# Six PSUM banks handed out one by one by a build-time scheduler, in place of two fixed PSUM pools, in a block-sparse attention and MLP kernel

## Chip, cores and metric

The kernel runs on one core of one Trainium2 chip. The metric is the device time of one execution in microseconds (us). One core has TensorE (PE; PEld is its weight load), VectorE (DVE), ScalarE (ACT), GpSimd (POOL) and SyncE (SP). PSUM is the memory that this kernel's matmuls write and that its VectorE and ScalarE instructions read. A run is called fast or slow by its clock and time; unless said otherwise, fast runs are compared with fast runs. Time before the change: 314.98 us in the first three runs.

## The reference, cut to what matters

```python
# attention: batch 4, 8 heads, sequence 768, head size 64, blocks of 32
scores = (q @ k.T) / 8
scores = where(block_mask, scores, -1e9)        # band, first/last blocks, sampled blocks
attn   = softmax(scores);  x = attn @ v          # -> x [4, 768, 512]
# residual MLP
a1  = alpha1 * x + beta1
u   = x + lam * (w_tok @ a1)                     # token mixing, 768 x 768
a2  = alpha2 * u + beta2
out = u + lam * (relu(a2 @ w_ch1) @ w_ch2)       # channel mixing, 512 -> 2048 -> 512
```

## The kernel before, as far as the change and the argument touch it

The kernel writes its program with a list scheduler that runs in Python while the kernel is built. Each piece of work is a `Job` with an engine, a guessed duration, a priority, and slots that it takes and gives back. The scheduler decides the order of instructions on every engine. A separate build tool then places the semaphore waits, and in the programs built here it placed them by tile (220 of 234 of PE's waits in the changed kernel, below).

Sixteen pairs of heads are processed. A PSUM bank is here 512 fp32 columns, as the kernel cuts it. A unit of scores is 128 x 1024 fp32, so it fills two banks. The scores of pairs 0 to 5 contract 88 rows (64 and 24 for the mask). Those of pairs 6 to 15 contract 64 rows, with the two heads of a pair side by side in rows 0 to 63 and 64 to 127 of the operands; in the trace of before the second head's matmul starts 3 to 4 ns after the first's (L729). The program uses eight PSUM banks:

```python
# two score tiles of 2 banks, two single tiles, one for channel mixing, one for attention @ v
def mm_tile(shape, dt=FP):
    return ps.tile(shape, dt, name="mm", tag="mm", bufs=2)
...
sps = ps.tile([P, UN], FP, name="sps", tag="sps", bufs=2)     # a new tile for every unit
...
slots = dict(sps=2, mm=2, cp=1, ops=1, eT=NET, ...)
...
# scores of pairs 6 to 15: always two units in one group
jq = Job("PE", 2 * 225.0 + 175.0, (1, i0), qk, deps, take=("sps", "sps"), give=give)
# exp of one unit frees its score tile
je = Job("ACT", 950.0, (1, i), ex, [qk_jobs[i]], take=("eT",), give=("sps",), lat=160.0)
# first channel matmul: a single product in an mm tile (later also half a score tile)
...
# scores may run ahead of channel mixing by LEAD units
def gated(j):
    return j.gate is not None and j.gate >= NS and j.gate - NS > st["ch"] / rate + LEAD
```

The softmax here doesn't subtract the row's maximum and nothing guards it: scores larger than these inputs give would overflow.

## Time and profile before

| what | before |
|---|---|
| time, median of the first 3 runs | 314.98 us (314.65 to 318.46) |
| PE busy | 305.6 us, 97% of the span |
| PE gaps (all pauses of PE together) | 5.2 us in 11 gaps |
| matmul streaming, columns / 2.4 + 2.7 ns each (a fit, below), summed | 290.3 us |
| what the start-to-start times add to that | 19.0 us |
| groups of 64-row scores | 45, all of two units |

The streaming sum and the excess were worked out from the start times of all 3197 matmuls; two heads that stream side by side count once. The form is a fit to this trace: the median from start to start is 56 ns at 128 columns and 216 ns at 512, so 160 ns for 384 columns, 2.4 columns a ns, and 2.7 ns more for each matmul. At 256 and 384 columns, with medians of 109 and 162 ns, the fit is off by less than 1 ns. Every matmul has its weight load here (3197 of each).

Lines of the page of the kernel before: busy time, then PE's busy tenths and the granted clock in 40 slices of the span.

```profile
span 314.2 us, 7579 instructions
...
PE 305.6 (97%) x3197; PEld 187.3 (60%) x3197; DVE 213.7 (68%) x447; ACT 198.1 (63%) x259; POOL 51.8 (16%) x91
...
PE   7999999988999999999999999999999999999995
...
PEclk9999999999999999999999999999999999999999
```

PE is the bottleneck. Its granted clock is 1.00 in the records from 6.0 to 313.2 us, and its last matmul ends at 310.7 us. (No record covers the first 6.0 us, in which the `warm` matmuls of 512 columns start 400 to 427 ns apart.) The two longest of PE's waits in the same kernel (who waited for whom: us in total, times, longest):

```profile
PE mm L946 <- DVE x_sb L874: 2.4, 1, 2.4
PE cp L170 <- DVE warm L165: 1.2, 1, 1.2
```

Timeline of before (start us, duration, engine, line, operation, count), one group of 64-row scores (L729):

```profile
152.08 1.03 PE L997 MATMUL cp<-w2b,hts 128*128 128x512 bf16 x4
153.04 0.61 PE L729 MATMUL sps<-qx,kx 64*128 64x256 bf16 x6
153.58 0.29 PE L787 MATMUL ops<-vext,eT 128*128 128x65 f16 x4
```

Four matmuls of 512 columns take 4 x 216 = 864 ns, so the scores could start at 152.94 us; they start 96 ns later. The scores themselves stream for 435 ns, with about 10 ns more after their first pair, and the next matmul starts 96 ns after that. The changes from 128-row to 64-row matmuls and back (mode changes, below) cost 95 and 96 ns at the median of the 45 groups, 0.19 us a group.

The second stretch lies after attention, where first channel products (L946) fill three PSUM tiles in turn:

```profile
267.08 0.81 PE L946 MATMUL sps<-uT,w1b 128*128 128x384 bf16 x4
267.73 1.46 PE L946 MATMUL mm<-uT,w1b 128*128 128x384 bf16 x8
267.93 0.58 ACT L959 ACTIVATE hts<-sps,b1t 128x384 bf16<-128x384 f32 x1
268.58 1.23 ACT L959 ACTIVATE hts<-mm,b1t 128x384 bf16<-128x384 f32 x2
269.03 0.49 PE L946 MATMUL sps<-uT,w1b 128*128 128x384 bf16 x2
```

Three products start between 267.08 and 269.03 us, one each 0.65 us.

### The profile page before, as it was taken

The numbers are of one execution on the slowest core, as the hardware profiler recorded it, in microseconds if no ns is written. First come the engines' busy times: TensorE is split into PE (matmuls) and PEld (weight loads), VectorE is DVE, ScalarE is ACT, GpSimd is POOL, SyncE is SP. The second block draws the span as 40 slices with busy tenths as digits, with TensorE's granted clock in tenths as the row PEclk, the third lists the DMA queues.
The fourth block names the chain that finished last, engine by engine and source line by source line (L and its number), as shares of the span: only waits on it lengthen the run. The fifth ranks groups of instructions, "written<-read, shape, count | busy, mean of one in ns | idle before, by whom it ended". The sixth has DMA issues, their size and how long they took to land.

```text
span 314.2 us, 7579 instructions
## 1 busy us (share of the span) xinstructions
PE 305.6 (97%) x3197; PEld 187.3 (60%) x3197; DVE 213.7 (68%) x447; ACT 198.1 (63%) x259; POOL 51.8 (16%) x91
## 2 busy tenths in 40 slices
PE   7999999988999999999999999999999999999995
PEld 3687888764645655566646655565656565556444
DVE  4599988859888687788869787788859671010111
ACT  4999988975768664766577654766587502828000
POOL 5647332000211220220310220230000000000000
PEclk9999999999999999999999999999999999999999
DMA  6999999994254564625452665626110203010021
GB/s 153 181 250 206 209 204 213 178 116 92 37 98 78 69 118 100 120 49 113 87 102 26 108 113 109 111 40 120 37 28 1 59 35 92 0 69 0 34 101 67
DMA packets 47210, 30.81 MB, mean 98 GB/s; under 512 B 27552, under 2 KB 43080, under 8 KB 47176
## 3 DMA queue, kind: packets, MB, share of 16 engines
q0 software_dynamic: 15984, 15.47, 31.4%
q1 hardware_dynamic: 30940, 14.61, 20.1%
q8 instruction: 25, 0.41, 0.6%
q10 hardware_dynamic: 252, 0.24, 0.2%
q14 instruction: 9, 0.07, 0.1%
HBM read 32.04 MB, written 6.33 MB: 122 GB/s over the span
## 4 chain that ended last, share of the span: by engine, by line
PE 79%; DMA 12%; issue 3%; DVE 3%; POOL 1%; ACT 1%; POOLq 0%
PE mm L946 23%; PE cp L997 22%; DMA v<-in_v_dram 8%; PE ops L787 8%; PE sps L729 7%; PE mm L864 7%; PE ops L997 5%; DMA q<-in_q_dram 4%; PE sps L946 2%; PE cp L170 2%; PE sps L651 2%; PE ops L691 1%; DVE ot L1014 1%; POOL w2b L389 0%; PE mm L218 0%
## 5 line engine op out<-in xcount | busy, mean ns | idle before, releaser
L755 ACT ACTIVATE eT<-sps 128x1024 f16<-128x1024 f32 x90 | 88.3, 1020 | 31.1 <-PE sps L729 28.8
L946 PE MATMUL mm<-uT,w1b 128*128 128x384 bf16 (+1 forms) x468 | 88.8, 326 | 3.0 <-DVE x_sb L874 2.4
L959 ACT ACTIVATE hts<-mm,b1t 128x384 bf16<-128x384 f32 x82 | 47.7, 582 | 49.3 <-PE mm L946 47.2
L997 PE MATMUL cp<-w2b,hts 128*128 128x512 bf16 (+1 forms) x320 | 76.9, 374 | 0.2
L946 PEld LDWEIGHTS <-w1b 128*128 128x128 bf16 x512 | 46.4, 97 | 34.9 <-issue 6.4
L760 DVE TENSOR_TENSOR eT<-eT,maskT 128x1024 f16<-128x1024 f16 x90 | 60.5, 685 | 4.1 <-ACT eT L755 4.0
L997 PEld LDWEIGHTS <-hts 128*128 128x128 bf16 x400 | 36.8, 98 | 35.7 <-issue 2.1
L666 ACT ACTIVATE eT<-sps 128x1024 f16<-128x1024 f32 (+1 forms) x55 | 52.1, 1024 | 3.1 <-PE sps L651 2.8
L787 PEld LDWEIGHTS <-eT 128*128 128x128 f16 x720 | 29.9, 97 | 15.9 <-issue 5.6
L1014 DVE TENSOR_TENSOR ot<-x_sb,cp 128x512 f32<-128x512 f32 (+1 forms) x20 | 13.5, 673 | 37.0 <-PE cp L997 36.8
L864 PE MATMUL mm<-a1p,wtokT 128*128 128x128 bf16 x576 | 36.2, 219 | 0.0
L787 PE MATMUL ops<-vext,eT 128*128 128x65 f16 x720 | 35.5, 194 | 0.0
L864 PEld LDWEIGHTS <-wtokT 128*128 128x128 bf16 x576 | 33.0, 98 | 2.0 <-issue 0.4
L651 PE MATMUL sps<-qx,kx 88*128 88x512 bf16 (+1 forms) x144 | 31.6, 325 | 0.6 <-DVE rel L213 0.5
L314 POOL COPY held<-flag 1x1 bf16<-1x1 bf16 x24 | 9.2, 385 | 131.1 <-DVE flag L334 131.1
L963 DVE TENSOR_SCALAR hts<-mm,b1t 128x384 bf16<-128x384 f32 x35 | 21.6, 616 | 13.5 <-PE mm L946 13.2
L729 PE MATMUL sps<-qx,kx 64*128 64x512 bf16 (+1 forms) x240 | 27.3, 327 | 0.0
L874 DVE TENSOR_TENSOR x_sb<-x_sb,mm 128x384 f32<-128x384 f32 x32 | 17.7, 552 | 4.7 <-PE mm L864 4.3
L691 PEld LDWEIGHTS <-eT 128*128 128x128 f16 x432 | 18.2, 97 | 4.4 <-DVE x_sb L626 0.6
L691 PE MATMUL ops<-vext,eT 128*128 128x65 f16 x432 | 20.2, 193 | 0.0
L626 DVE TENSOR_TENSOR x_sb<-ops,rcp 128x384 f32<-128x384 f32 x32 | 17.9, 558 | 1.1
L729 PEld LDWEIGHTS <-kx 64*128 64x128 bf16 x240 | 8.1, 94 | 16.5 <-issue 14.1
(71 smaller groups left out, 237.2 us busy)
## 6 DMA issues: line engine op xcount, KB each, us to landing
out_dram<-ot SPq DMA_DIRECT2D x23, 256.0 KB
v<-in_v_dram POOLq DMA_DIRECT2D x16, 192.0 KB, 5.4
q<-in_q_dram POOLq DMA_DIRECT2D x15, 192.0 KB, 3.9
k<-in_k_dram POOLq DMA_DIRECT2D x15, 192.0 KB, 5.4
w1b<-in_moe_w_ch_dram POOLq DMA_DIRECT2D x4, 512.0 KB, 10.3
w2b<-in_moe_w_ch_dram POOLq DMA_DIRECT2D x4, 512.0 KB, 16.4
wtk<-in_moe_w_tok_dram POOLq DMA_DIRECT2D x3, 384.0 KB, 10.3
maskT<-mask_rows SPq DMA_DIRECT2D x14, 72.0 KB
```

The source lines that it names most:

```text
L651: nc.tensor.matmul(sps[:, f - u * UN : f - u * UN + w], kx[h][0:KC, ts(jt, P)], qx[h][0:KC, c : c + w], start=True, stop=True,)
L666: nc.scalar.activation(eT[:, c], sps[:, c], AF.Exp, bias=EXPB, scale=SCALE)
L691: nc.tensor.matmul(ops[p, a][:, t * VW : t * VW + D + 1], eTs[p, u][:, ts(i - u * GU, P)], vx[:, a, jt, 0 : D + 1], start=(i % HT == 0), s ...
L729: nc.tensor.matmul(sps[:, a * 512 + lo : a * 512 + lo + w], kx[sl][r, ts(jt, P)], qx[sl][r, c : c + w], start=True, stop=True,)
L755: nc.scalar.activation(eT[:], sps[:], AF.Exp, bias=EXPB, scale=SCALE)
L760: nc.vector.tensor_tensor(out=e, in0=e, in1=maskT[:, u, :].unsqueeze(1).broadcast_to([P, 2, 512]), op=ALU.min,)
L787: nc.tensor.matmul(ops[p, a][:, t * VW : t * VW + D + 1], eTs[p, u][:, a * 512 + c * P : a * 512 + (c + 1) * P], vx[:, a, jt, 0 : D + 1], ...
L864: nc.tensor.matmul(tp[:, j, :], wtokT[:, s, ts(3 * g + j, P)], tl["a1p", p][:, s, :], start=(s == 0), stop=(s == NT - 1),)
L946: nc.tensor.matmul(hp[:, 0:nc_], w1b[:, dk, ts(f, P)], uTs[b][:, dk, hf * HS : hf * HS + nc_], start=(dk == 0), stop=(dk == 3),)
L959: nc.scalar.activation(hts[kk][:, f, :], hp[:, 0:HS], AF.Relu, bias=b1t[:, f : f + 1], scale=1.0)
L963: nc.vector.tensor_scalar(out=hts[kk][:, f, :], in0=hp[:, 0:HS], scalar1=b1t[:, f : f + 1], scalar2=0.0, op0=ALU.add, op1=ALU.max,)
L997: nc.tensor.matmul(cps[kk, mi][:, 0:w], hts[kk][:, nk, ts(m, P)], w2tile[0][:, nk, lo : lo + w], start=(nk == 0), stop=(nk == 15),)
```

## The change

The intent: with 64-row scores in groups of three units instead of two, there are fewer mode changes. Three units need six banks, so all six banks that are neither `cp` nor `ops` become one shared store. The scheduler knows them as `b0` to `b5`, gives single products one bank and scores a pair of banks, and holds single products back for a moment when a third pair would come free, as long as PE has 800 ns of other work (`COVER`).

```diff
-LEAD = 15
+LEAD = 18
+COVER = 800.0
...
-    def mm_tile(shape, dt=FP):
-        return ps.tile(shape, dt, name="mm", tag="mm", bufs=2)
+    ps6 = ps.tile([P, 6 * 512], FP, name="ps6", tag="ps6", bufs=1)
+    BANKS = tuple(f"b{i}" for i in range(6))
+    PAIRS = ("b0+b1", "b2+b3", "b4+b5")
+
+    def bank(name, shape, dt=FP):
+        t = ps6[:, ts(BANKS.index(name), 512)]
+        ...
+    def two_banks(names):
+        return ps6[:, ts(PAIRS.index(names), UN)]
...
-        sps=2, mm=2, cp=1, ops=1, eT=NET, ...
+        **{b: 1 for b in BANKS}, cp=1, ops=1, eT=NET, ...
...
-                sps = ps.tile([P, UN], FP, name="sps", tag="sps", bufs=2)
+                sps = two_banks(tl.pop(("spsb", p, u)))
...
+    def qk_group(n, banks):              # n = 2 or 3 units, as free pairs allow
+        ...
+        j = Job("PE", n * 225.0 + 175.0, (1, i0), qk, (), take=take, give=give)
...
+                    hold[1] = not n or later
+                    hold[0] = n > m and not later and other_work(t) >= COVER
```

More of the change, by code (lines that the diff above doesn't have):

```diff
@@ L145, in pair_ap @@
         return src[b, 2 * n : 2 * n + 2].rearrange("h (p o) d -> p h (o d)", o=NT)
-    def mm_tile(shape, dt=FP):
-        return ps.tile(shape, dt, name="mm", tag="mm", bufs=2)
+    ps6 = ps.tile([P, 6 * 512], FP, name="ps6", tag="ps6", bufs=1)
[3 more added lines that the diff above has]
+        t = ps6[:, ts(BANKS.index(name), 512)]
+        if dt != FP:
+            t = t.bitcast(dt)
+        t = t[:, 0 : int(np.prod(shape[1:]))]
+        return t if len(shape) == 2 else t.rearrange("p (o c) -> p o c", o=shape[1])
+    def two_banks(names):
+        return ps6[:, ts(PAIRS.index(names), UN)]
     q2f = wk.tile([P, 2, NT * D], FP, name="q2f", tag="hts", bufs=2)
@@ L213, in first_cast, with transposes @@
                 nc.vector.tensor_copy(out=dst, in_=sl)
-    def transposes(rel, a, slots=range(NT)):
-        tps = mm_tile([P, NT, P], BF)
+    def transposes(rel, a, name, slots=range(NT)):
+        tps = bank(name, [P, NT, P], BF)
         for o in slots:
             nc.tensor.transpose(tps[:, o, :], rel[:, a, o, :], identb[:])
-        return tps[:].rearrange("p o c -> p (o c)")
+        return tps.rearrange("p o c -> p (o c)")
     first_cast(0)
     block_mask()
-    flatA = transposes(rel0, 0, range(0, 3))
-    flatB = transposes(rel0, 0, range(3, 6))
+    flatA = transposes(rel0, 0, "b0", range(0, 3))
+    flatB = transposes(rel0, 0, "b1", range(3, 6))
     bqs = []
-    for w, tag in ((0, "sps"), (1, "ops")):
-        t = ps.tile([P, UN if tag == "sps" else 512], FP, name=tag, tag=tag, bufs=2 if tag == "sps" else 1)
+    for w in range(2):
+        t = ps.tile([P, 512], FP, name="ops", tag="ops", bufs=1) if w else bank("b2", [P, 512])
         nc.tensor.matmul(
@@ L253 @@
     slots = dict(
-        sps=2, mm=2, cp=1, ops=1, eT=NET, head=NQB, vext=NV, ld=NLD, rel=3,
+        **{b: 1 for b in BANKS}, cp=1, ops=1, eT=NET, head=NQB, vext=NV, ld=NLD, rel=3,
         x=NXB, uT=3, hts=2, a1p=2, ub=2, ot=2, w2b=1,
@@ L272, in __init__ @@
             self.gate = None
+            self.marks = []
             self.n = len(jobs)
@@ L423, in tr @@
         def tr(t=t):
-            tl["wt", t] = tp = mm_tile([P, NT, P], BF)
+            tl["wt", t] = tp = bank(tl.pop(("wtb", t)), [P, NT, P], BF)
             for s in range(NT):
@@ L428, in cp_ @@
         def cp_(eng, t=t):
-            copy(eng, wtokT[:, :, ts(t, P)], tl.pop(("wt", t))[:])
-        j = Job("PE", mmt(NT, P), (5, t), tr, [wload["tok", t // 2]], take=("mm",))
+            copy(eng, wtokT[:, :, ts(t, P)], tl.pop(("wt", t)))
+        j = Job("PE", mmt(NT, P), (5, t), tr, [wload["tok", t // 2]], take=((BANKS, ("wtb", t)),))
         last = t == NT - 1
         wtok_jobs.append(
-            Copy((4, t), cp_, [j], give=("mm", "w2b") if last else ("mm",), only=False)
+            Copy((4, t), cp_, [j], give=(("wtb", t),) + (("w2b",) if last else ()), only=False)
         )
@@ L525, in f_tr @@
             def f_tr():
-                tl["h0"] = transposes(rel0, 1)
+                tl["h0"] = transposes(rel0, 1, tl.pop(("h0b",)))
             def f_cq(eng):
@@ L535 @@
             j = Job("DVE", 720.0, (2, 0), fc)
-            j = Job("PE", mmt(NT, P), (2, 0), f_tr, [j], take=("mm",))
+            j = Job("PE", mmt(NT, P), (2, 0), f_tr, [j], take=((BANKS, ("h0b",)),))
             j = Copy((1, 0, 1), f_cq, [j, head_ready[0]], take=("head",), only=3 >= 0)
-            j = Copy((1, 0, 2), f_ck, [j], give=("mm", "rel"), only=3 >= 0)
+            j = Copy((1, 0, 2), f_ck, [j], give=(("h0b",), "rel"), only=3 >= 0)
             def f_mb():
@@ L561, in tr @@
                 def tr(p=p, a=a, h=h):
-                    tl["hd", h] = transposes(rels[p], a)
+                    tl["hd", h] = transposes(rels[p], a, tl.pop(("hdb", h)))
                 def cpq(eng, h=h):
@@ L568, in cpk @@
                     copy(eng, kx[h % NQB][0:D, :], tl["hd", h][D:P, :])
-                jt = Job("PE", mmt(NT, P), (2, p, a), tr, [ck, prev], take=("mm", "head"),
+                jt = Job("PE", mmt(NT, P), (2, p, a), tr, [ck, prev], take=((BANKS, ("hdb", h)), "head"),
                          give=("rel",) if a else ())
@@ L573 @@
                 j2 = Copy((1, p, a), cpk, [jt], only=p <= 3)
-                prev = head_ready[h] = Job("NONE", 0.0, (0,), lambda: None, [j1, j2], give=("mm",), lat=0.0)
+                prev = head_ready[h] = Job("NONE", 0.0, (0,), lambda: None, [j1, j2], give=(("hdb", h),), lat=0.0)
         else:
@@ L611 @@
     pv_last = {}
-    grp = []
-    exps = []
     min_jobs = {}
@@ L673, in single @@
             give = ("head",) if u in (NU // 2, NU - 1) else ()
-            jq = Job("PE", mmt(2, 512) + (8 if u % 3 != 1 else 8), (1, i), qk, deps, take=("sps",), give=give)
+            jq = Job("PE", mmt(2, 512) + (8 if u % 3 != 1 else 8), (1, i), qk, deps, take=((PAIRS[1:], ("spsb", p, u)),), give=give)
             jq.gate = i
             qk_jobs[i] = jq
-            exp_jobs[i] = je = Job("ACT", 950.0, (1, i), ex, [jq], take=("eT",), give=("sps",), lat=160.0)
+            exp_jobs[i] = je = Job("ACT", 950.0, (1, i), ex, [jq], take=("eT",), give=(("spsb", p, u),), lat=160.0)
             lo, hi = u * GU, (u + 1) * GU
@@ L715, in paired @@
         b, n = pairs[p]
-        mins = []
         for u in range(NU):
-            i = p * NU + u
-            grp.append((p, u))
-            if len(grp) == 2:
-                def qk(units_=tuple(grp)):
-                    for pp_, u_ in units_:
-                        sps = ps.tile([P, UN], FP, name="sps", tag="sps", bufs=2)
-                        sl = slot_of(pp_)
-                        for lo, jt, c, w in pieces(u_):
-                            for a in range(2):
-                                r = slice(a * D, (a + 1) * D)
-                                nc.tensor.matmul(
-                                    sps[:, a * 512 + lo : a * 512 + lo + w],
-                                    kx[sl][r, ts(jt, P)],
-                                    qx[sl][r, c : c + w],
-                                    start=True,
-                                    stop=True,
-                                )
-                        tl["sps", pp_, u_] = sps
-                        st["qk"] += 1
-                give = sum((("head",) for _, u_ in grp if u_ == NU - 1), ())
-                deps = [head_ready[2 * pp_] for pp_, _ in grp]
-                i0 = grp[0][0] * NU + grp[0][1]
-                deps.append(qk_jobs[i0 - 1])
-                jq = Job("PE", 2 * 225.0 + 175.0, (1, i0), qk, deps, take=("sps", "sps"), give=give)
-                jq.gate = i
-                for pp_, u_ in grp:
-                    qk_jobs[pp_ * NU + u_] = jq
-                grp.clear()
+            qk_jobs[p * NU + u] = Job((), 0.0, (1, p, u), None)
         for u in range(NU):
@@ L762, in mn @@
                 )
-            exps.append((p, u, ex, mn))
-        while exps and (exps[0][0] * NU + exps[0][1]) in qk_jobs:
-            p_, u, ex, mn = exps.pop(0)
-            i = p_ * NU + u
-            je = Job("ACT", 950.0, (1, i), ex, [qk_jobs[i]], take=("eT",), give=("sps",), lat=160.0)
-            min_jobs[i] = Job("DVE", 690.0, (1, i), mn, [je] + mask_jobs)
-            if u == NU - 1:
-                pv_of(p_)
+            exp_jobs[i] = je = Job("ACT", 950.0, (1, i), ex, [qk_jobs[i]], take=("eT",), lat=160.0)
@@ new lines, in paired, with single_bank, other_work, free_pairs @@
+            min_jobs[i] = Job("DVE", 690.0, (1, i), mn, [je] + mask_jobs)
+        pv_of(p)
+    def single_bank(j):
+        return any(isinstance(t, tuple) and t[0][0] == "b0" for t in j.take)
+    def other_work(t):
+        return sum(
+            j.dur * (3 if j.prio[0] == 6 else 1)
+            for r, j in by_eng["PE"]
+            if r <= t and j.done is None and not single_bank(j) and can(j)
+        )
+    def free_pairs():
+        return [x for x in PAIRS if slots[x[:2]] and slots[x[3:]]]
@@ new lines, in heads_of_next, with qk @@
+    def heads_of_next(t):
+        i0 = st["qk"]
+        n = 0
+        while i0 + n < n_units and n < 3:
+            d = head_ready[2 * units[i0 + n][0]].done
+            if d is None or d > t:
+                break
+            n += 1
+        return n if n == 3 or n == n_units - i0 or n == 2 else 0
+    def qk_group(n, banks):
+        i0 = st["qk"]
+        us = units[i0 : i0 + n]
+        banks = banks[-n:]
+        def qk():
+            for k_, (p, u) in enumerate(us):
+                sps = two_banks(banks[k_])
+                sl = slot_of(p)
+                for lo, jt, c, w in pieces(u):
+                    for a in range(2):
+                        r = slice(a * D, (a + 1) * D)
+                        nc.tensor.matmul(
+                            sps[:, a * 512 + lo : a * 512 + lo + w],
+                            kx[sl][r, ts(jt, P)],
+                            qx[sl][r, c : c + w],
+                            start=True,
+                            stop=True,
+                        )
+                tl["sps", p, u] = sps
+                st["qk"] += 1
+                exp_jobs[i0 + k_].give = (banks[k_][:2], banks[k_][3:])
+        take = tuple(b for x in banks for b in (x[:2], x[3:]))
+        give = tuple("head" for _, u in us if u == NU - 1)
+        j = Job("PE", n * 225.0 + 175.0, (1, i0), qk, (), take=take, give=give)
+        jobs.pop()
+        j.gate = i0 + n - 1
+        for k_ in range(n):
+            j.marks.append((90.0 + 225.0 * (k_ + 1), qk_jobs[i0 + k_]))
+        return j
@@ L860, in tok @@
             def tok(p=p, g=g):
-                tl["tp", p, g] = tp = mm_tile([P, 3, P])
+                tl["tp", p, g] = tp = bank(tl.pop(("tpb", p, g)), [P, 3, P])
                 for j in range(3):
@@ L873, in xadd @@
                 sl = x_sb[:, s0 + 3 * g : s0 + 3 * g + 3, 2 * n * D : (2 * n + 2) * D]
-                nc.vector.tensor_tensor(out=sl, in0=sl, in1=tl.pop(("tp", p, g))[:], op=ALU.add)
+                nc.vector.tensor_tensor(out=sl, in0=sl, in1=tl.pop(("tp", p, g)), op=ALU.add)
             def ubm(p=p, g=g, n=n, s0=s0):
@@ L883, in ubm @@
                 )
-            jt = Job("PE", mmt(18, P), (3, p, g), tok, a_jobs + wtok_jobs, take=("mm",),
+            jt = Job("PE", mmt(18, P), (3, p, g), tok, a_jobs + wtok_jobs, take=((BANKS, ("tpb", p, g)),),
                      give=("a1p",) if g else ())
-            jx = Job("DVE", 555.0, (1, p, g), xadd, [jt], give=("mm",))
+            jx = Job("DVE", 555.0, (1, p, g), xadd, [jt], give=(("tpb", p, g),))
             ubs.append(Job("DVE", 555.0, (2, p, g), ubm, [jx, l_a2], take=("ub",) if g == 0 else ()))
@@ L898, in utr @@
             def utr(p=p):
-                tl["up", p] = up = mm_tile([P, NT, P], BF)
+                tl["up", p] = up = bank(tl.pop(("upb", p)), [P, NT, P], BF)
                 for t in range(NT):
@@ L903, in ucp @@
             def ucp(eng, p=p, n=n, ut_tile=ut_tile):
-                copy(eng, ut_tile()[:, n, 0:S], tl.pop(("up", p))[:].rearrange("p o c -> p (o c)"))
-            j = Job("PE", mmt(NT, P), (2, p, 9), utr, ubs, take=("mm",), give=("ub",))
-            ut_jobs[p] = Copy((1, p, 9), ucp, [j], take=take, give=("mm",))
+                copy(eng, ut_tile()[:, n, 0:S], tl.pop(("up", p)).rearrange("p o c -> p (o c)"))
+            j = Job("PE", mmt(NT, P), (2, p, 9), utr, ubs, take=((BANKS, ("upb", p)),), give=("ub",))
+            ut_jobs[p] = Copy((1, p, 9), ucp, [j], take=take, give=(("upb", p),))
         else:
@@ L939, in c1 @@
                     hts[kk] = wk.tile([P, 16, HS], BF, name="hts", tag="hts", bufs=2)
-                if tl.pop(("mmsel", kk, f)) == "sps":
-                    hp = ps.tile([P, UN], FP, name="sps", tag="sps", bufs=2)
-                else:
-                    hp = mm_tile([P, 512])
+                hp = bank(tl.pop(("mmsel", kk, f)), [P, 512])
                 tl["hp", kk, f] = hp
@@ L974 @@
                 deps.append(first)
-            take = ((("mm", "sps"), ("mmsel", kk, f)),) + (("hts",) if f == 0 else ())
+            take = ((BANKS, ("mmsel", kk, f)),) + (("hts",) if f == 0 else ())
             j = Job("PE", mmt(4, HS), (5, kk, f), c1, deps, take=take,
@@ L993, in c2 @@
                         tag = tl.pop(("cpsel", kk, mi))
-                        shape = [P, UN] if tag == "sps" else [P, DM]
-                        cps[kk, mi] = ps.tile(shape, FP, name=tag, tag=tag, bufs=2 if tag == "sps" else 1)
+                        cps[kk, mi] = bank(tag, [P, DM]) if tag in BANKS else ps.tile([P, DM], FP, name=tag, tag=tag, bufs=1)
                     for nk in range(4 * r, 4 * r + 4):
@@ L1005 @@
                 deps = relus[4 * r : 4 * r + 4] + w2_jobs[2 * r : 2 * r + 2] + ([prev] if prev else [])
-                take = ((("cp", "ops", "sps") if kk == 2 * B - 1 else ("cp", "ops"), ("cpsel", kk, mi)),) if r == 0 else ()
+                take = ((("cp", "ops") + (BANKS if kk == 2 * B - 1 else ()), ("cpsel", kk, mi)),) if r == 0 else ()
                 prev = Job("PE", mmt(4, w), (6, kk, mi, r), c2, deps, take=take,
@@ L1044, in can @@
                 ok = False
+                if opts is BANKS:
+                    if hold[0]:
+                        return False
+                    opts = sorted(BANKS, key=lambda x: (not owned[other(x)], x))
+                    if st["qk"] < NPE * NU:
+                        opts = BANKS[:2]
+                    elif not hold[1] and any(owned.values()):
+                        opts = [x for x in BANKS if owned[x] or owned[other(x)]]
                 for o in opts:
-                    if o == "sps" and not attention_over():
+                    if o[0] == "b" and opts[0] == "cp" and not attention_over():
                         continue
@@ L1051, in can @@
                         continue
-                    if slots[o] > 0:
+                    if min(slots[x] for x in o.split("+")) > 0:
                         ok = o
@@ L1063, in gated, with other @@
         return j.gate is not None and j.gate >= NS and j.gate - NS > st["ch"] / rate + LEAD
+    hold = [False, False]
+    owned = {x: 0 for x in BANKS}
+    def other(x):
+        return BANKS[BANKS.index(x) ^ 1]
     by_eng = {e: [] for e in free_at}
@@ L1097 @@
                     continue
+                hold[:] = [False, attention_over()]
+                n = 0
+                if e == "PE" and NPE * NU <= st["qk"] < n_units:
+                    n = heads_of_next(t)
+                    fp_ = free_pairs()
+                    m = min(n, len(fp_))
+                    later = n and gated(qk_group(n, []))
+                    hold[1] = not n or later
+                    hold[0] = n > m and not later and other_work(t) >= COVER
                 for r, j in by_eng[e]:
@@ L1105 @@
                         best = (key, j)
+                if n and m >= min(2, n) and (
+                    not best or not later and not hold[0] and best[0] > (False, (1, st["qk"]))
+                ):
+                    best = (None, qk_group(m, fp_))
                 if best is None:
@@ L1112 @@
                         o = chosen[tk[1]]
-                        slots[o] -= 1
+                        for x in o.split("+"):
+                            slots[x] -= 1
+                        if o in owned:
+                            owned[o] = 1
                         tl[tk[1]] = o
@@ L1145 @@
                 heapq.heappush(events, (j.done, seq, j))
+                for off, m in j.marks:
+                    m.done = t + off + DRAIN + SEM
+                    seq += 1
+                    heapq.heappush(events, (m.done, seq, m))
                 if e == "PE":
@@ L1155 @@
                     by_eng[e2] = [x for x in by_eng[e2] if x[1] is not j]
-                left -= 1
+                left -= max(1, len(j.marks))
                 moved = True
@@ L1172 @@
                 if isinstance(g, tuple):
-                    slots[tl.pop(("slot", g))] += 1
+                    for x in tl.pop(("slot", g)).split("+"):
+                        slots[x] += 1
+                        if x in owned:
+                            owned[x] = 0
                 else:
```

## The prediction

> **What bounds it now.** The busy table has TensorE (PE) at 97% of 314.2 us, VectorE 68%, ScalarE 63%; the chain that ended last is 79% PE. The 20 us windows from 20 us on show PE at 19.7 to 20.0 us, except 60 to 80 us (17.4). So only PE time counts. Start-to-start times of matmuls in the trace fit columns/2.4 GHz + 2.7 ns within 2 ns. The sum is 290.3 us of streaming and 19.0 us of excess. Its largest part: around the scores of pairs 6 to 15 (two heads at once, 64 rows each, L729) each change from 128-row to 64-row matmuls costs 96 ns, and each change back another 96. With 45 groups of two units that is 45 x 0.19 = 8.6 us. [...] Second: at 69.5 us PE stands still for 2.4 us (waits view), because a channel matmul's PSUM tile is released by a VectorE add (L874) that queued behind a copy waiting for a late load of v.
>
> **What the change does.** The matmul work is the same. The two fixed PSUM pools become six banks that the build-time scheduler hands out. Up to pair 5 the split stays 4 + 2, so the first 69 us should hardly move. From pair 6 on a group can have three units when all three bank pairs are free; single products (token mixing, first channel matmul) are held back for that while PE has other work as cover. Attention's lead grows from 15 to 18 units.
>
> **Costing.** All groups of three: 30 groups, saving 15 x 0.19 = 2.9 us, the ceiling. A group of three needs every single drained first (bias and relu 0.58 to 0.62 us plus latency), and exp releases one pair per 1.02 us. Per three units there are about 3.7 singles and 2.2 us of value and second-channel work to cover: feasible, not always. I estimate 22 threes and 12 twos: 34 groups, saving 11 x 0.19 = 2.1 us, all on the critical path. The 2.4 us wait may go, since other banks open when the last 88-row scores are issued, but the scheduler prefers the same two there: I count -0.7 us. Singles held back and exps in bursts of three (3.1 us of ScalarE) should bring new short PE waits: +0.5 us. The 60 us after attention gain nothing. Sum: -2.3 us.
>
> **Predicted: 312.7 us**, 80% range 310.2 to 315.0. Chances: faster by over 2% 0.03, within 2% 0.94, slower 0.03.
>
> **What would show each step.** (1) Groups of L729 in the timeline: 33 to 37 instead of 45; the switch stays 96 ns each way. (2) Streaming sum about 290 us, clock unchanged. (3) Waits view: the L874 wait shrinks or stays; new waits of first-channel matmuls under 1 us in total. (4) ScalarE's 23 waits for scores become fewer. (5) The time after the last score stays 62 to 68 us.
>
> **What would make it wrong.** If the scheduler's timing model is off in the new arrangement, PE stalls on bank releases eat the 2 us or more. If the 2.4 us wait disappears and nearly all groups are threes, it is 310 or below. If the merged PSUM tensor makes coarser waits than separate tiles, it is slower.

The sum is -2.1 - 0.7 + 0.5 = -2.3 us, from 314.98 to 312.7.

## The result

| | before | changed |
|---|---|---|
| time, median of 4 runs each | 315.22 us (314.65 to 318.46) | 597.15 us (592.41 to 607.07) |
| ratio of fast runs | | 1.885 (95%: 1.866 to 1.905) |
| span of the profiled run | 314.2 us | 595.8 us |
| granted TensorE clock | 0.998 | 0.813 |
| PE gaps | 5.2 us in 11 | 190.6 us in 223 |
| streaming sum of all matmuls at full clock | 290.3 us | 290.3 us |
| groups of 64-row scores | 45 of two | 24 of two, 14 of three |

A ratio is the mean time of one kernel's fast runs over that of the other's in the same rounds, so it is not quite the ratio of the medians. One of the four runs of the changed kernel, 607.07 us, was slow; it is in the median and not in the ratio.

The same lines of the page, now of the changed kernel:

```profile
span 595.8 us, 7614 instructions
...
PE 401.8 (67%) x3197; PEld 233.9 (39%) x3197; DVE 211.0 (35%) x434; ACT 214.3 (36%) x272; POOL 52.2 (9%) x91
...
PE   6766655666666665766676767666766666758587
...
PEclk7555665555756567899899879998999799999999
```

Nothing is the bottleneck: every engine idles about a third of the time or more, all through the span. That includes the first slices, where the schedule was hardly meant to change, and the last ones, where there are no scores at all. So one should not look for the cause in the groups of scores. The waits of PE, five of its longest groups:

```profile
PE ps L973 <- ACT eT L736: 42.5, 39, 2.1
PE ps L663 <- ACT eT L678: 36.2, 36, 1.8
PE ps L973 <- ACT hts L986: 29.3, 44, 1.1
PE ps L894 <- ACT eT L736: 16.7, 16, 1.2
PE ps L784 <- ACT hts L986: 10.2, 19, 1.4
```

These are short waits, but many. They pair things that need not meet: a first channel product (L973) waits for an exp (L736) that reads scores. The place to see it is after attention, where first channel products (now L973) are alone with their bias and relu (L986):

```profile
525.30 0.81 PE L973 MATMUL ps<-uT,w1b 128*128 128x384 bf16 x4 [0.67 <-ACT hts L986]
526.15 0.58 ACT L986 ACTIVATE hts<-ps,b1t 128x384 bf16<-128x384 f32 x1 [0.90 <-PE ps L973]
526.78 0.81 PE L973 MATMUL ps<-uT,w1b 128*128 128x384 bf16 x4 [0.67 <-ACT hts L986]
527.63 0.58 ACT L986 ACTIVATE hts<-ps,b1t 128x384 bf16<-128x384 f32 x1 [0.90 <-PE ps L973]
```

Here the scheduler has six banks to choose from, and yet PE and ScalarE take turns as if there were one: a product each 1.48 us (525.30, 526.78) in place of 0.65 us. Six banks worked as one.

**How the build tool sees it.** In the built program every wait can be followed to the instruction that ends it. A reader is an instruction of ScalarE or VectorE that reads a bank. Of the 234 waits of PE instructions for a reader of the six banks, 220 were for a reader of *another* bank, 14 for one of their own. It is not the number of waits that is wrong: with own-bank waits there are 241 (e1 below). But each is for the last reader of any bank, and not for an earlier one of its own. Slices of this one tile were, for its waits, the whole tile. In the kernel before each use had its own tile, so the question never arose. The scheduler's book said six banks; the tool's book said one tile.

**Where the 281.6 us went** (span 595.8 less 314.2, from the two traces). PE gaps grew by 190.6 - 5.2 = 185.4 us. For 222 us the granted clock was half, and the matmuls that started in that time stream 73.3 us at full clock; at half clock they take about as much again, +73.3 us (median from start to start 107 ns in place of 56 at 128 columns, 427 in place of 216 at 512). Together that is 259 us. The remaining 23 us I have not split. I take the half clock for a second-order effect of the pauses: in these runs it comes with them (190.6 us of gaps and a clock of 0.813 here), and where they are fewer it is nearly gone (5.2 us and 0.998 before, 33.7 us and 0.999 in e4; 0.994 in e1).

### The profile page after: what moved, and what is told of

The parts are those of the page before. It is cut to its first block, busy times and chain, and to the rows that moved or that the text cites. A ratio compares the mean times of both kernels' runs of the same rounds, so it can differ in the third digit from the quotient of the medians.

```text
span 595.8 us, 7614 instructions
## 1 busy us (share of the span) xinstructions
PE 401.8 (67%) x3197; PEld 233.9 (39%) x3197; DVE 211.0 (35%) x434; ACT 214.3 (36%) x272; POOL 52.2 (9%) x91
## 4 chain that ended last, share of the span: by engine, by line
PE 54%; ACT 32%; DVE 9%; issue 4%; DMA 1%; ACTq 0%; DVEq 0%
PE ps L973 19%; ACT eT L736 14%; ACT eT L678 9%; PE ps L663 8%; ACT hts L986 8%; PE ps L894 8%; PE cp L1023 6%; PE ps L784 5%; DVE x_sb L904 3%; PE ops L1023 3%; DVE hts L990 2%; PE ops L817 2%; PE ps L231 1%; DVE qx L294 1%; DVE kx L294 1%
## 5 line engine op out<-in xcount | busy, mean ns | idle before, releaser
L973 PE MATMUL ps<-uT,w1b 128*128 128x384 bf16 (+1 forms) x512 | 115.5, 358 | 88.5 <-ACT eT L736 42.5
L736 ACT ACTIVATE eT<-ps 128x1024 f16<-128x1024 f32 x90 | 90.1, 1022 | 88.9 <-PE ps L784 39.0
L973 PEld LDWEIGHTS <-w1b 128*128 128x128 bf16 x512 | 52.8, 104 | 141.4 <-issue 120.5
L986 ACT ACTIVATE hts<-ps,b1t 128x384 bf16<-128x384 f32 x106 | 59.5, 579 | 132.1 <-PE ps L973 107.6
L678 ACT ACTIVATE eT<-ps 128x1024 f16<-128x1024 f32 (+1 forms) x55 | 55.3, 1008 | 101.7 <-DVE kx L294 19.7
L663 PE MATMUL ps<-qx,kx 88*128 88x512 bf16 (+1 forms) x144 | 50.7, 483 | 45.3 <-ACT eT L678 36.2
L894 PE MATMUL ps<-a1p,wtokT 128*128 128x128 bf16 x576 | 48.7, 254 | 24.0 <-ACT eT L736 16.7
L904 DVE TENSOR_TENSOR x_sb<-x_sb,ps 128x384 f32<-128x384 f32 x32 | 17.7, 554 | 78.1 <-PE ps L894 31.0
L663 PEld LDWEIGHTS <-kx 88*128 88x128 bf16 x144 | 18.0, 127 | 62.4 <-issue 58.6
L784 PE MATMUL ps<-qx,kx 64*128 64x512 bf16 (+1 forms) x240 | 27.2, 335 | 13.2 <-ACT hts L986 10.2
L990 DVE TENSOR_SCALAR hts<-ps,b1t 128x384 bf16<-128x384 f32 x22 | 13.6, 618 | 52.6 <-PE ps L973 24.6
```

What stands on the lines that cost most here:

```text
L663: nc.tensor.matmul(sps[:, f - u * UN : f - u * UN + w], kx[h][0:KC, ts(jt, P)], qx[h][0:KC, c : c + w], start=True, stop=True,)
L678: nc.scalar.activation(eT[:, c], sps[:, c], AF.Exp, bias=EXPB, scale=SCALE)
L736: nc.scalar.activation(eT[:], sps[:], AF.Exp, bias=EXPB, scale=SCALE)
L784: nc.tensor.matmul(sps[:, a * 512 + lo : a * 512 + lo + w], kx[sl][r, ts(jt, P)], qx[sl][r, c : c + w], start=True, stop=True,)
L894: nc.tensor.matmul(tp[:, j, :], wtokT[:, s, ts(3 * g + j, P)], tl["a1p", p][:, s, :], start=(s == 0), stop=(s == NT - 1),)
L904: nc.vector.tensor_tensor(out=sl, in0=sl, in1=tl.pop(("tp", p, g)), op=ALU.add)
```

## The experiments

Theory A: one PSUM tensor makes every access wait for all earlier ones, and the schedule is innocent. Theory B: the new schedule (single products held back, groups of three, free choice of banks) starves PE. The order of instructions of e1, e4, e9 and e10 on all five engines is that of the changed kernel, that of e2 and e3 is that of the kernel before (compared in the built programs). All results were correct.

| run | waits of PE for readers: own bank / another bank | time, median | ratio to before (95%) |
|---|---|---|---|
| changed kernel | 14 / 220 | 597.15 | 1.885 (1.866 to 1.905) |
| e1 changed, own-bank waits | 241 / 0 | 311.61 | 0.987 (0.982 to 0.993) |
| e2 order of before, one tensor | 2 / 209 | 594.61 | 1.882 (1.872 to 1.893) |
| e3 order of before, one tensor, own-bank waits | 236 / 1 | 314.32 | 0.995 (0.990 to 0.999) |
| e4 changed, three tensors of two banks | 144 / 68 | 348.64 | 1.103 (1.098 to 1.108) |
| e9 changed, only readers against readers freed | 13 / 221 | 558.48 | 1.765 (1.752 to 1.778) |
| e10 changed, only PE against readers freed | 241 / 0 | 341.13 | 1.082 (1.078 to 1.086) |
| e11 changed, six tensors, exps split | 341 / 0 | 313.45 | 0.996 (0.990 to 1.001) |

The unchanged kernel had medians of 315.82, 314.80 and 315.03 us (e1 to e4, e5 to e8, e9 to e11).

### e1: the same order, waits for own banks alone

The build tool lets a program say that an instruction does not depend on others of a group. After the program is written, every access to the six banks names the accesses it really depends on, and is freed of the rest:

```diff
+def own_banks(nc, tc, name="ps6"):
+    wrote, read, others = {}, {}, {}
+    for ins in list(nc.cur_bb.bb.instructions):
+        here, other = ...          # banks of ps6 and other tensors that ins touches
+        ...
+        # keep: last writer and reader of each own bank, and whatever shares another tensor
+        tc.declare_no_dep(ins, group=name, keep=list(keep.values()), reason="another bank")
+        tc.add_to_no_dep_group(name, ins)
+        ...
+    own_banks(nc, tc)
     pin_order(nc, tc)
```

> The changed kernel with the same instructions in the same order on every engine; only the waits differ: an access to the six-bank tensor waits for earlier accesses to its own banks alone. In the built program 220 of 234 waits of TensorE on readers of the six banks were for a reader of another bank; here none is. Theory A (one PSUM tensor makes every access wait for all earlier ones): 309 to 316 us, clock above 0.99, TensorE waits under 8 us in all. Theory B (the new schedule itself, with single products held back and groups of three, starves TensorE): 550 us or more, as the changed kernel.

Measured: 311.61 us median (310.55 to 313.96, 4 runs), ratio 0.987. Lines of its page:

```profile
span 312.2 us, 7556 instructions
...
PE 301.6 (97%) x3162; PEld 189.7 (61%) x3197; DVE 207.7 (67%) x434; ACT 206.8 (66%) x272; POOL 53.6 (17%) x91
...
PE   7999999998999999999999999999999999999995
...
PEclk9999999997999999999999999999999999999999
```

The whole loss is gone, with every instruction where it was. (35 of the 3197 matmul records are missing from this trace, so its busy sum is a little low. The profiled run is the slowest of the four; the 7 in its clock is a single stretch of 3.4 us at half clock.) Theory B cannot explain that. The first channel products after attention again run back to back; one line of its timeline covers six and a half of them, and ScalarE reads at the same time:

```profile
261.81 4.39 PE L1016 MATMUL ps<-uT,w1b 128*128 128x384 bf16 x26
261.84 4.48 ACT L1029 ACTIVATE hts<-ps,b1t 128x384 bf16<-128x384 f32 x7
```

### e2: the kernel before, on one tensor

```diff
+    ps6 = ps.tile([P, 6 * 512], FP, name="ps6", tag="ps6", bufs=1)
+    turn = dict(mm=0, sps=0)
-        return ps.tile(shape, dt, name="mm", tag="mm", bufs=2)
+        t = ps6[:, ts(turn["mm"] % 2, 512)]; turn["mm"] += 1; ...
-                sps = ps.tile([P, UN], FP, name="sps", tag="sps", bufs=2)
+                sps = sps_tile()        # ps6[:, ts(1 + turn % 2, UN)]
```

> The kernel before in its own order of instructions, with its two score tiles and two single tiles placed as slices of one six-bank tensor, nothing else. Theory A: 480 to 680 us, clock 0.75 to 0.9, though no line of the schedule changed (209 of 211 of TensorE's waits on readers of these banks are for another bank). Theory B: 313 to 318 us, as before.

Measured: 594.61 us (592.06 to 597.89). The order is that of before, the loss that of the change:

```profile
span 591.6 us, 7567 instructions
...
PE 396.7 (67%) x3160; PEld 231.2 (39%) x3197; DVE 215.8 (36%) x447; ACT 207.7 (35%) x259; POOL 51.9 (9%) x91
...
PEclk8555555565655887899998998899999989999999
```

Its PE gaps are 191.5 us, those of the changed kernel 190.6. So the single tensor is enough for the loss without the new schedule (e2), and without its waits for other banks the new schedule loses nothing (e1).

### e3: control, the order of before on one tensor with own-bank waits

The two edits above together.

> Control: the merged tensor in the order of before, with waits narrowed to own banks. Both theories: 314 to 317 us. Anything else would mean that narrowing the waits, or the fixed addresses, has an effect of its own, and the first run could not be read as meant.

Measured: 314.32 us (313.71 to 314.40), ratio 0.995 (0.990 to 0.999). Two lines of its page:

```profile
PE 302.5 (97%) x3160; PEld 187.0 (60%) x3197; DVE 213.7 (68%) x447; ACT 198.5 (64%) x259; POOL 51.8 (17%) x91
...
PEclk9999999999999999999999999999999999999999
```

So narrowed waits and fixed addresses have little effect of their own, though perhaps not none: the interval ends just below 1. Of e1's gain, 0.2 to 3 us could be of this kind rather than of the schedule. I did not separate this further.

### e4: three tensors of two banks

```diff
-    ps6 = ps.tile([P, 6 * 512], FP, name="ps6", tag="ps6", bufs=1)
+    ps2 = [ps.tile([P, UN], FP, name=f"psd{i}", tag=f"psd{i}", bufs=1) for i in range(3)]
```

> The changed kernel, same order, with three tensors of two banks instead of one of six; the build's own waits. 68 of 212 of TensorE's waits on readers are then still for the neighbour bank of the pair. Theory A: most of the loss is gone, 325 to 420 us. Theory B: 550 us or more.

Measured: 348.64 us (347.62 to 349.40), inside the range. With 68 waits left for another bank, 33 to 37 us are left of the loss:

```profile
PE 308.7 (89%) x3162; PEld 190.9 (55%) x3197; DVE 207.7 (60%) x434; ACT 204.4 (59%) x272; POOL 52.7 (15%) x91
...
PEclk9999999999999999999999999999999999999999
```

PE gaps are 33.7 us, about 28 us more than before (a little too many, since matmul records are missing here too), and the clock is 0.999, so none of this loss is clock and most of it is waiting. Between these two runs the loss grows faster than the number of such waits: 68 of them cost about 0.5 us each, 220 of them 1.3 us each, clock included.

### e9 and e10: which false order costs

Two kinds of order come from the one tensor: PE against the readers, and the readers (ScalarE, VectorE) against each other, since reads by two engines are also kept in turn (74 such waits for another bank in e10). e9 frees only the second kind, e10 only the first. In e1's loop this is one added rule each:

```diff
 e9:  for a PE instruction keep all earlier readers, for a reader all earlier PE instructions
+        for x in past[not pe][-400:]:
+            keep[x.name] = x
 e10: for a reader keep all earlier readers
+            for x in past[-40:]:
+                keep[x.name] = x
```

> The changed kernel, same order; the waits between TensorE and the readers of the six banks stay as the build made them (221 of 234 of TensorE's waits on readers, and 162 of 237 of the readers' waits on TensorE, are for another bank), and only the order between ScalarE's and VectorE's reads of different banks is dropped. If the loss comes from TensorE taking turns with the readers: 520 to 600 us. If it comes from the two readers taking turns with each other: under 380 us.

> The reverse: TensorE and the readers wait for their own banks alone, but ScalarE and VectorE stay ordered against each other over all six banks (74 such waits for another bank). TensorE-against-readers: 312 to 335 us. Readers against each other: 500 us or more.

Measured: e9 558.48 us (551.68 to 564.63; its profiled run, 564.63, was slow, so no line of that profile is used); e10 341.13 us (340.30 to 341.21). PE against the readers is the bulk: 558.5 less 311.6 is 247 us with this kind alone. The readers against each other cost 29.5 us alone (e10), which I had guessed at 0 to 23, and 39 us on top of the other kind (597.2 less 558.5). The lines in e10 that show it, from VectorE's waits:

```profile
DVE hts L1038 <- ACT eT L784: 12.3, 12, 1.2
...
DVE qx L342 <- ACT eT L726: 10.5, 8, 3.9
```

A relu on VectorE (L1038) waits for an exp on ScalarE that reads other banks. In e5 below, where readers are free, this pair is not among VectorE's seven longest waits, the last of which is 3.4 us.

### e11: a plain repair, six tensors of one bank

No declarations: each bank is its own tile, and an exp, which would read across two tiles, is split in two.

```diff
-    ps6 = ps.tile([P, 6 * 512], FP, name="ps6", tag="ps6", bufs=1)
+    psb = [ps.tile([P, 512], FP, name=f"psb{i}", tag=f"psb{i}", bufs=1) for i in range(6)]
...
-                nc.scalar.activation(eT[:], sps[:], AF.Exp, bias=EXPB, scale=SCALE)
+                for c in (slice(0, 512), slice(512, UN)):
+                    nc.scalar.activation(eT[:, c], sps[:, c], AF.Exp, bias=EXPB, scale=SCALE)
```

> A plain repair with the build's own waits: six tensors of one bank each, the order of the changed kernel, and each exp of two banks split into two of one bank, which costs ScalarE 2 x 593 - 1022 = 164 ns a unit, 24 us in all (the 593 ns is the shortest exp of 512 columns in the profile of before). ScalarE is at 63%, so I expect TensorE to hide most of it: 311 to 319 us. If ScalarE's extra time delays bank releases, up to 330 us.

Measured: 313.45 us (312.12 to 314.62), ratio 0.996 (0.990 to 1.001). One sees the price on ScalarE, while PE stays at 97%:

```profile
PE 300.8 (97%) x3162; PEld 189.5 (61%) x3197; DVE 207.6 (67%) x434; ACT 214.1 (69%) x415; POOL 53.2 (17%) x91
```

ScalarE has 415 instructions in place of 272. Its busy time is 7 us above e1's 206.8 us, not the 24 us of my estimate, which added up durations. The group of the later exps shows why (busy time, mean ns of one):

```profile
L746 ACT ACTIVATE eT<-psb 128x512 f16<-128x512 f32 x180 | 92.6, 606 | 27.0 <-PE psb L794 21.1 <-issue 5.0 <-PE ops L827 0.9
```

180 times 606 ns are 109 us, but they keep ScalarE busy for 92.6 us only: the two halves overlap. The 90 whole exps of e1 took 87.0 us. This repairs the loss with the build tool's own waits, but a gain over before is no longer clear of the noise.

### e5 to e8: was the idea of the change right?

With the waits repaired, the question of the prediction can be asked after all: do groups of three pay? All four have own-bank waits. In all four the edit of e1 is in place (e5 is e1 once more). The further edits:

```diff
 e6: at most two units in a group
-        while i0 + n < n_units and n < 3:
+        while i0 + n < n_units and n < 2:
 e7: always hold single products back
-COVER = 800.0
+COVER = 0.0
 e8: the lead of before
-LEAD = 18
+LEAD = 15
```

> The changed kernel with own-bank waits once more, as the reference point of this call (38 score groups: 24 of two, 14 of three units): 310 to 313 us, 1.0 to 1.6% under the kernel before.

> Own-bank waits, six banks, but at most two units in a group: 45 groups. If a mode change into and out of a group costs 0.19 us and that is the gain of threes, this is slower than the reference point by 7 x 0.19 = 1.3 us (0.4 to 2.2). If the groups of three gain nothing (the gain over before comes from banks that are free to choose), the two agree within 0.4 us.

> Own-bank waits; single products are held back for a third pair of banks even where TensorE has little else to do (cover of 0 in place of 800 ns): 19 groups of three and 16 of two, 35 in all. The mode changes alone would give 3 x 0.19 = 0.6 us less than the reference point; if the cover was needed, new TensorE waits outweigh it and it is the same or up to 2 us slower. My guess: within 1 us of the reference point.

> Own-bank waits, lead of attention back at 15 units: 20 groups of three and 15 of two, 35 in all. If only the number of groups counts: 0.6 us faster than the reference point. If the longer lead is what keeps TensorE fed, it is slower by 0.5 to 3 us.

| run | groups of three / two | time, median | ratio to before (95%) | excess at mode changes: bare + waits | excess before first 64-row group | other excess |
|---|---|---|---|---|---|---|
| before | 0 / 45 | 314.80 | | 8.6 + 0.4 | 7.6 | 2.5 |
| e5 reference point | 14 / 24 | 311.65 | 0.991 (0.986 to 0.996) | 7.3 + 0.3 | 8.5 | 1.5 |
| e6 twos only | 0 / 45 | 315.88 | 1.004 (0.999 to 1.009) | 8.6 + 1.2 | 7.6 | 4.5 |
| e7 always hold | 19 / 16 | 314.75 | 0.998 (0.994 to 1.002) | 6.9 + 5.0 | 4.9 | 3.5 |
| e8 lead 15 | 20 / 15 | 315.08 | 0.999 (0.995 to 1.004) | 6.7 + 3.3 | 8.1 | 1.7 |

The excess columns are us of the one profiled execution: start-to-start times less streaming, split by where they fall ("bare" is at most 97 ns a change; e7 also has one group of a single unit). All five streaming sums are 290.3 to 290.5 us.

One thing in this table can mislead. The profiled runs of e5, e6 and e7 were each the slowest of their six, 2.6 to 3.0 us over the median, and each has one stretch of 3.4 us at half clock that starts at 72 to 74 us; those of before and e8 have none while PE works. It costs 1.5 to 1.8 us of streaming, which stands in the excess, and in e5 it starts at the end of one long wait of PE (2.0 us). The profiled run of the kernel before had that wait too (2.4 us) and no such stretch. So fast runs fall in two kinds: e5's are 311.07 to 311.87 us at a clock of 0.999 or 1.0, and 314.41 and 314.61 us at 0.993 and 0.995. With runs at 0.998 and above alone, the medians are 314.5 (before), 311.3, 315.4, 314.7 and 315.1 us, so e5 stays the fastest and e6 the slowest.

The bare mode changes behave as costed: 7 groups fewer are 1.3 us (e5 against before, 7.3 against 8.6). But my expectations for e6 and e7 did not hold, and of e8's two branches neither did by the medians (3.4 us slower; the second branch had 0.5 to 3). e6 is 4.2 us slower than e5 where I had 1.3. In its profile the waits at mode changes and the other excess are 3.9 us larger and the start is 0.9 us shorter, some 0.5 us of both only because the half clock falls elsewhere. The rest looks like new waits in the rearranged schedule; I have not followed it to single causes. e7 and e8 have two or three groups fewer than e5 and 0.4 to 0.6 us less of bare changes, and are 3.1 and 3.4 us slower by the medians (2.5 us each by the means of six): more waits at the very places where groups begin and end, 3.3 to 5.0 us against 0.3. In e7 one of them is for a load:

```profile
PE ps L827 <- DMA kx<-rel: 3.0, 1, 3.0
```

So the number of groups is not the measure. As far as these profiles show, a group of three must not only be formed but must find its banks and inputs ready on the chip when the scheduler's model says so. In these runs the settings of the change (18 units, 800 ns) did so best, by some 3 us. Whether that is a rule or luck of three settings stays open.

## Why the prediction was wrong

Predicted 312.7 us, range 310.2 to 315.0; measured 597.15 us.

1. *"The two fixed PSUM pools become six banks that the build-time scheduler hands out."* This is the step that failed. It takes the banks as independent because the scheduler treats them so. The waits come from the tool that places semaphores, and for it the slices were one tensor: 220 of 234 waits of PE for readers were for another bank. The term missing from the sum is +281.6 us of span: 185.4 us of PE gaps, 73.3 us of half clock, 23 us not split. e1 and e2 show it from both sides.
2. *"If the merged PSUM tensor makes coarser waits than separate tiles, it is slower."* The right risk stood in the last line, with no size and a share of 0.03. Its size could have been estimated from the trace of before: a product that must alternate with its relu costs about 0.65 + 0.58 us plus the two handovers, not 0.65 (1.48 us were measured in the changed kernel), and 1605 of the 3197 matmuls of the bottleneck engine write those banks. A yes-or-no question on which a factor of two hangs should have widened the range.
3. *"The matmul work is the same"*, *"streaming sum about 290 us"*: right, 290.3 us in both. *"Clock unchanged"*: wrong, 0.813.
4. *"The first 69 us should hardly move"*: wrong. The first 64-row score came at 194.4 us in place of 74.2, since single products, transposes and scores of all pairs share the tensor.
5. *"The switch stays 96 ns each way"*: right (95 to 96 ns in e5). *"34 groups, saving 11 x 0.19 = 2.1 us"*: mis-sized. There were 38 groups, and the bare changes fell by 1.3 us.
6. *"The 2.4 us wait may go ... I count -0.7 us"*: it stayed; in e5 PE waits for the same VectorE add 2.4 us in two pieces (in e1 1.8 us in one).

```profile
PE ps L1016 <- DVE x_sb L947: 2.4, 2, 2.0
```

7. *"new short PE waits: +0.5 us"* and *"ScalarE's 23 waits for scores become fewer"*: with repaired waits there was no such loss in e5 (other excess 1.5 against 2.5 us), and ScalarE's waits for 64-row scores rose from 23 to 30 at nearly the same total (28.8 and 28.4 us). The longer bursts did not show as expected. The waits, before and in e5:

```profile
ACT eT L755 <- PE sps L729: 28.8, 23, 3.8
ACT eT L779 <- PE ps L827: 28.4, 30, 2.6
```

8. *"The time after the last score stays 62 to 68 us"*: it was 105.6 us, and with repaired waits 70.8 us, just outside, against 67.6 us before.

With the waits repaired the kernel takes 311.6 us, inside the predicted range and 1.1 us under the predicted time, in both (e1, e5). That is what the sum of the prediction was about, but the kernel that was handed over is not that kernel, and the agreement is partly of terms that missed in opposite directions. It is also the one version here whose gain on before is clear of the noise in two calls, 0.9 and 1.3% (the interval of e3, run once, ends just below 1), which is under the 2% at which a difference is called faster.

## What to carry to other kernels

A scheduler that hands out slices of one PSUM tile manages only its own book; in the programs built here the semaphore waits followed the tiles that the build tool knew (220 of 234 were for another bank, and none once the waits were declared by bank). Give each unit of reuse its own tile, or follow a few waits of the built program to their producers before trusting the schedule. In the changed kernel's profile the mark of the false order was lockstep: two engines in turn (PE 0.67 us and ScalarE 0.90 us idle in each 1.48 us), waits between operations that share no data (42.5 us of L973 for the exps of L736), and no engine busy for more than 67% of the span, with all stages slow, those included that the change should not touch.

## What these runs measured of the hardware

- PSUM guarded by bank: e1 and e5, whose results were correct, have no wait of PE for a reader of another bank (241 for its own in e1). The price of guarding by whole tensor was a factor of 1.88 (e2), and 29.5 us for merely keeping ScalarE's and VectorE's reads of different banks in turn (e10).
- Mode changes: 95 to 96 ns each way between 128-row and 64-row matmuls (medians of 45 changes each way in before); between 128-row and 88-row matmuls nothing was added at the median (50 changes each way, 0 and -1 ns against the fit).
- The clock: in the changed kernel no PE gap is longer than 2.15 us, and yet the clock fell to half 13 times before its last matmul had ended and was there for 222 of 596 us. Before each fall, PE was busy for 18 to 49% of the preceding 3.4 us (the shortest stretch at half clock here is 3.41 us); before each rise, for 80 to 100% (matmul ends are modelled, so these shares are rough). These are no thresholds: 3.4 us with PE 30% busy, up to 361.4 us, brought no fall. A stretch in lockstep at 0.81 us busy in each 1.48 us, 55%, stayed at full clock.
